# A dilated convolution with gate: a third level of differences for the V common part, the S part per oct, XB tiles by shifting, and another order of the units

## The chip, the core and the metric

The kernel runs on one core of one Trainium2 chip. The metric is the device time of one execution in microseconds. The kernel before takes 330.51 us (median of 3 runs, 329.73 to 330.65).

## The reference

The input x is 2 x 16000 x 144 (B x T x D) in bf16. A causal convolution with 15 taps and dilation 2 maps the 144 channels to 288; the first 144 of these go through tanh and the other 144 through a sigmoid, the two are multiplied, and the product is multiplied with a 144 x 144 matrix.

```python
pad = (K - 1) * dil                      # 28
xp = jnp.pad(x, ((0, 0), (pad, 0), (0, 0)))
h = sum over i of einsum('btc,cd->btd', xp[:, pad - 2 * i : pad - 2 * i + T, :], w[i])   # K = 15 taps
f, g = h[..., :D], h[..., D:]
z = jnp.tanh(f) * sigmoid(g)
return z @ w_o
```

(The loop over the taps is written as one line here.)

## The kernel before

**Tiles.** The 32000 time steps are laid out as 128 partitions of 250 consecutive steps (L = 250). A "tile" e is the set of the 128 steps that have the same place e in their partition, so one matmul with a 128x128 tile as its stationary operand gives 128 outputs for the 288 columns of a tap. Tap i at tile e needs tile e - 2i. Eight tiles make an oct; there are 31 octs and two steps before them. The first 128 channels of x are the A part: XA[slot, i] is tile i of an oct, transposed (channels on the partitions). The other 16 channels are the B part: one XB tile holds the 16 channels of eight tiles (e, e - 4, e - 8 and so on, 16 partitions each), so that two matmuls with the weights WB do the B part of all 15 taps.

**Fewer matmuls by differences.** Plain code would need 15 + 2 matmuls for each tile. The kernel uses a scheme in the manner of Winograd or Karatsuba: it forms sums of weights once (WS, WC, WT, WD, by `wsum`, line 655) and differences of tiles on VectorE, and combines the partial results. Of an oct it forms V and D(D) (first and second differences between tiles of even and odd place and neighbouring octs; `ef` and `vdiff`), DU (differences of XA, `diff`), BD (differences of XB); all of these go through line 709. For a pair of octs (o0 = 2m + 1, o1 = 2m + 2) `g_diffs` (line 774) forms differences between octs: GX of XA, GU of DU (both line 783), and GD of D (line 790).

**Units.** The main loop runs over 30 units (m, r), with 15 pairs m and r = 0, 1. A unit gives eight output tiles, four for each oct of the pair (h = 0, 1). Its parts, each with its matmuls on TensorE (all go through the helper at line 795), are:

- CD (line 979, k = 0, 1): common part from D with the weights WD, 8 matmuls in all; ScalarE evicts it to UD (k = 0) or UC (k = 1).
- XC (k = 0, 1): common part from DU with WT, 4 matmuls; ScalarE copies the result to a second PSUM bank (`copy`, line 937).
- XR (k = 0, 1): adds GU and XB parts for each oct, 12 matmuls; for k = 0 VectorE adds UD and writes UE (line 964, kept in the memory of Xp), for k = 1 ScalarE evicts to XS.
- UP (line 972, h = 0, 1): GpSimd adds UC and XS to UX (line 974). It also waits for an instruction of EF that is kept in TRIG.
- SC: the half that the S part of both octs shares, from XA with WT, 2 matmuls, and one copy to the other oct's bank.
- SR (h = 0, 1): adds the GX parts, 4 matmuls, and one copy each to the bank for the second half of the columns' pair.
- EF (line 1010, h = 0, 1): adds 4 V tiles in each of two banks, 16 matmuls; then four adds on VectorE (line 1023), two with UE into new banks, two with UX in place.
- DD (line 1028; h, part): adds the GD and BD parts, 23 matmuls in all; then `finish_pair`: sigmoid and tanh on ScalarE into TS (lines 472 and 475), the product on VectorE into Z (line 823).

That is 69 matmuls a unit. For each oct, `ship` (line 873) has the DMA transpose Z to ZT (line 878), `project` (PJ in the order; matmuls at line 895) multiplies by w_o in three groups, ScalarE evicts to OS (line 899), and a DMA stores it (line 905).

**Order.** Inside a unit the parts are issued in the order of the string `ORDER` (line 17). In it EF and DD belong to the present unit, and XC, CD, XR, SC, SR, UP to the next one; PJ takes the next group from a list. A list scheduler, `_Graph.schedule`, then plans all engines with a duration given for each operation, may move TensorE's groups forward within a window of `PE_WIN` = 14 groups, and gives out the 8 PSUM banks. VectorE operations and GpSimd's UX that are marked `lock` are kept from overlapping in the plan. The engines then run the planned order with semaphore waits.

**Loading.** For two pairs ahead, `stage` loads the x rows in chunks of 16 tiles (`load_xchunk`, Xr, three buffers). `load_xa` (line 672) copies the 128 A channels of an oct from Xr to a staging tile STA (on ScalarE up to oct 4, line 677, then on VectorE, line 680), and SP issues a DMA transpose to XA (line 682). `compact_chunk` copies the 16 B channels of a chunk into XBc, ordered so that the window of an XB tile is contiguous; `load_xb` (line 685) copies the eight windows of an oct to STB (line 698) and SP issues a DMA transpose to XB (line 700). STA and STB have one buffer each. XB has six slots of an oct, XA nine. All these DMAs are issued by SP, in the planned order.

Before the first unit, the outputs of the first tiles are computed directly with 17 matmuls each.

Of the kernel before, what the change touches and what calls it, by code (L numbers as in the profile page):

```python
# [16 lines left out]
ORDER = "EF0 DD01 PJ XC1 DD00 CD1 CD0 XR1 XC0 EF1 PJ SC UP1 DD10 XR0 PJ SR0 SR1 UP0 DD11"  # L17
# [357 lines left out]
def _conv_wavenet_kernel(nc, x, w, w_o, out):  # L375
# [17 lines left out]
    MB = (NE_ALL + 2) // 4 + 1  # L393
# [8 lines left out]
    NX = 3  # L402
# [7 lines left out]
    NST = 1  # L410
# [3 lines left out]
    STA_ACT = 4  # L414

    with contextlib.ExitStack() as st:
# [5 lines left out]
        XBc = sb("XBc", [NP, 4, MB, DB], BF16)  # L422
        STA = sb("STA", [NP, NST, 8, 128], BF16)
        STB = sb("STB", [NP, NST, 8, 128], BF16)
# [16 lines left out]
        GX = sb("GX", [NP, NG, 2, 2, 128], BF16)  # L441
# [3 lines left out]
        XS = sb("XS", [NP, 1, 2, N2], F32)  # L445
        UD = sb("UD", [NP, NUD, 2, N2], F32)
# [5 lines left out]
        WD = sb("WD", [NP, 4, 2, N2], BF16)  # L452
        Z = sb("Z", [NP, NZ, 8 * D], BF16)
# [113 lines left out]
        def cmp_op(eng, src, e0, e1, keys_r, tag, dur):  # L567

            m0, nm = (e0 + 2) // 4, (e1 - e0) // 4
            def f(v):  # L570
                s = src.rearrange("p (m c) d -> p c m d", c=4)
                dst = bass.AP(XBc[:].tensor, (MB - 1 - m0) * DB, [[4 * MB * DB, NP], [MB * DB, 4], [-DB, nm], [1, DB]])
                if eng == "act":
                    return v.activation(dst, s, ACT.Copy)
                return v.tensor_copy(dst, s)
# [9 lines left out]
        def compact_pro(pi):  # L585
            e0, e1 = pro_pieces[pi]
            if pi == 0:
                def f2(a):
                    s = Xp[:, 0:2, DA:D]
                    dst = bass.AP(XBc[:].tensor, 2 * MB * DB + (MB - 1) * DB, [[4 * MB * DB, NP], [MB * DB, 2], [1, DB]])  # L590
# [37 lines left out]
        def b_halo():  # L628
# [6 lines left out]
            def fix(p):  # L635
                s = Xp[:, H:E0, DA:D]
                dst = bass.AP(XBc[:].tensor, 2 * MB * DB + (MB - 1 - H // 4) * DB, [[4 * MB * DB, NP], [MB * DB, 2], [1, DB]])
                return p.tensor_copy(dst, s)
            g.add("pool", fix, r=xp_keys[2], w=hk, dur=0.3)
            for o, tiles, bb in ((-1, range(E0 - 4, E0), 7), (0, range(E0, E0 + 8), 6)):  # L640
                fns = []
                for e in tiles:
# [5 lines left out]
                      r=[("bank", HB[bb])], w=[("XB", bslot(o))], dur=0.5 if o < 0 else 0.95)  # L648
# [17 lines left out]

        def compact_chunk(ci):
            a, c = CH[ci]
            s = ci % NX
            cmp_op("dve", Xr[:, s, 0:c - a, DA:D], E0 + a, E0 + c, [("Xr", s)], ("XBc", ci), 0.16 + (c - a) * DB / 1900.0)  # L670

        def load_xa(o):
            s, q = aslot(o), o % NST
            ci = chunk_of(8 * o)
            i0 = 8 * o - CH[ci][0]
            if o <= STA_ACT:
                g.add("act", lambda a: a.activation(STA[:, q, :, :], Xr[:, ci % NX, i0:i0 + 8, 0:DA], ACT.Copy),
                      r=[("Xr", ci % NX)], w=[("STA", q)], dur=0.95, prio=2)
            else:
                g.add("dve", lambda v: v.tensor_copy(STA[:, q, :, :], Xr[:, ci % NX, i0:i0 + 8, 0:DA]),  # L680
                      r=[("Xr", ci % NX)], w=[("STA", q)], dur=0.34, lock=True)
            g.add("sp", lambda e: e.dma_start_transpose(XA[:, s, :, :], STA[:, q, :, :].rearrange("p a b -> p (a b)")),
                  r=[("STA", q)], w=[("XA", s)], dur=1.3, dma="xa", nbytes=8 * 128 * 128 * 2)

        def load_xb(o):
            s, q = bslot(o), o % NST
            e0 = E0 + 8 * o
            ck = set()
            for e in range(e0 - 28, e0 + 8):
                if e >= EP:  # L690
                    ck.add(("XBc", chunk_of(e - E0)))
                else:
                    ck.update(hk5 + ["XBcz"])
            m4 = (e0 + 2) // 4

            def cp(v):
                src = bass.AP(XBc[:].tensor, (MB - 1 - m4) * DB, [[4 * MB * DB, NP], [-DB, 2], [MB * DB, 4], [1, 128]])
                return v.tensor_copy(STB[:, q, :, :].rearrange("p (h c) b -> p h c b", h=2), src)  # L698
            g.add("dve", cp, r=sorted(ck, key=str), w=[("STB", q)], dur=0.34, lock=True)
            g.add("sp", lambda e: e.dma_start_transpose(XB[:, s, :, :], STB[:, q, :, :].rearrange("p a b -> p (a b)")),  # L700
                  r=[("STB", q)], w=[("XB", s)], dur=1.3, dma="xb", nbytes=8 * 128 * 128 * 2)

        def xbk(o):
            return [("XB", bslot(o))]
# [590 lines left out]
```

## Time and profile before

| | |
|---|---|
| median of 3 runs | 330.51 us |
| the profiled execution | 331.81 us |
| its span, first to last instruction | 330.1 us |
| TensorE, VectorE, ScalarE, GpSimd busy | 319.2, 305.6, 255.7, 107.2 us |
| weight loads busy | 250.4 us |
| mean granted TensorE clock | 0.998 |
| HBM read, written | 11.82, 9.22 MB |

The profile comes from one execution; the 1.7 us between its time and its span lie ahead of the first and behind the last instruction. "Busy" is the union of an engine's instructions; matmuls are pipelined, so that one is drawn 286 ns long while the next starts after about 122 ns. In the views PE is TensorE, PEld its weight loads, DVE VectorE, ACT ScalarE, POOL GpSimd, SP the engine that issues the DMAs; L795 is line 795 of the kernel. An arrow "<-" behind idle time names what ended it.

### The profile page before, as it was taken

What the parts mean: (1) busy time and instruction counts of PE and PEld (TensorE: products, weight loads), DVE (VectorE), ACT (ScalarE), POOL (GpSimd) and SP (SyncE); (2) the same over time, 40 slices, a digit from 0 to 9 for tenths busy, and PEclk for the clock granted to TensorE, in tenths of its full rate; (3) what the DMA queues carried; (4) which work ended last, traced back from release to release, by engine and by line L of the source; (5) the groups of instructions that cost most, each with busy time, mean ns of one, the idle gap of its engine ahead of it and who ended that gap; (6) DMA issues with size and microseconds to landing.
All of it is one profiled execution on the core that took longest, in us unless ns stands there. A gap on an engine that the chain in (4) does not pass through costs nothing. (4 is left out here: it accounts for less than half of the span.)

```text
span 330.1 us, 7585 instructions
## 1 busy us (share of the span) xinstructions
PE 319.2 (97%) x2701; PEld 250.4 (76%) x2701; DVE 305.6 (93%) x713; ACT 255.7 (77%) x786; POOL 107.2 (32%) x89
## 2 busy tenths in 40 slices
PE   7999799999999999999999999999999999999995
PEld 7877577888876778886788888887678878777873
DVE  2989899999999999999999999999999999999671
ACT  4455597898877878887789888877878788888875
POOL 7840333333213332223434322333312334331320
PEclk9999999999999999999999999999999999999999
DMA  8989714869475595838649495666847176463254
GB/s 205 320 129 201 182 32 113 199 101 193 108 151 138 135 174 126 175 113 148 168 84 224 103 164 157 135 167 137 171 106 161 51 160 105 104 134 73 71 75 143
DMA packets 111587, 46.51 MB, mean 141 GB/s; under 512 B 102766, under 2 KB 105247, under 8 KB 111549
## 3 DMA queue, kind: packets, MB, share of 16 engines
q1 hardware_dynamic: 111033, 45.68, 62.9%
q8 instruction: 21, 0.34, 0.5%
q0 software_dynamic: 512, 0.33, 0.4%
q14 instruction: 17, 0.14, 0.1%
q10 hardware_dynamic: 4, 0.01, 0.0%
HBM read 11.82 MB, written 9.22 MB: 64 GB/s over the span
## 5 line engine op out<-in xcount | busy, mean ns | idle before, releaser
L974 POOL TENSOR_TENSOR UX<-UC,XS 128x576 f32<-128x576 f32 x60 | 91.1, 1539 | 204.7 <-DVE PS L1023 166.9
L795 PE MATMUL PS<-WA,GD 128*128 128x288 bf16 x450 | 89.2, 286 | 2.5 <-DVE PS L1023 2.4
L795 PE MATMUL PS<-WB,BD 128*128 128x288 bf16 x240 | 67.4, 286 | 0.0
L795 PE MATMUL PS<-WC,V 128*128 128x288 bf16 x420 | 66.2, 286 | 0.2 <-ACT PS L937 0.2
L937 ACT ACTIVATE PS<-PS 128x288 f32<-128x288 f32 x150 | 58.5, 402 | 9.8 <-DVE Xp L964 3.4
L899 ACT ACTIVATE OS<-PS 128x432 bf16<-128x432 f32 (+1 forms) x91 | 44.4, 490 | 27.6 <-PE PS L895 26.4
L475 ACT ACTIVATE TS<-PS 128x144 bf16<-128x144 f32 x272 | 56.9, 298 | 8.6 <-PE PS L795 7.6
L1023 DVE TENSOR_TENSOR PS<-PS,Xp 128x288 f32<-128x288 f32 x120 | 53.6, 459 | 3.8 <-PE PS L795 2.8
L795 PEld LDWEIGHTS PS<-WA,GD 128*128 128x128 bf16 x450 | 40.6, 98 | 17.4 <-DVE PS L1023 5.5
L1023 DVE TENSOR_TENSOR PS<-PS,UX 128x288 f32<-128x288 f32 x120 | 49.8, 455 | 0.2
L795 PEld LDWEIGHTS PS<-WC,V 128*128 128x128 bf16 x420 | 40.9, 98 | 10.7 <-ACT PS L937 0.5
L472 ACT ACTIVATE TS<-PS 128x288 bf16<-128x288 f32 x114 | 39.8, 420 | 9.4 <-PE PS L795 9.2
L895 PE MATMUL PS<-WOR,ZT 128*128 128x144 bf16 (+1 forms) x333 | 44.5, 253 | 2.1 <-DVE Xp L964 2.0
L964 DVE TENSOR_TENSOR Xp<-PS,UD 128x576 f32<-128x576 f32 x60 | 43.0, 749 | 1.5 <-PE PS L795 1.1
L795 PE MATMUL PS<-WS,GU 128*128 128x288 bf16 x210 | 44.4, 286 | 0.0
L823 DVE TENSOR_TENSOR Z<-TS 128x288 bf16<-128x288 bf16 x125 | 36.7, 302 | 4.3 <-ACT TS L475 3.2
L795 PE MATMUL PS<-WB,XB 128*128 128x288 bf16 x140 | 37.6, 286 | 0.0
L895 PEld LDWEIGHTS PS<-WOR,ZT 128*128 128x128 bf16 x333 | 28.7, 98 | 9.5 <-DVE Xp L964 2.6
L795 PE MATMUL PS<-WD,DD 128*128 128x288 bf16 x210 | 34.6, 286 | 0.0
L709 DVE TENSOR_TENSOR BD<-XB 128x1024 bf16<-128x1024 bf16 (+1 forms) x35 | 28.6, 819 | 0.0
L795 PEld LDWEIGHTS PS<-WB,BD 128*128 128x128 bf16 x240 | 23.5, 98 | 5.7
L795 PE MATMUL PS<-WT,DU 128*128 128x288 bf16 x120 | 24.6, 286 | 0.9 <-DVE Xp L964 0.5
(85 smaller groups left out, 449.9 us busy)
## 6 DMA issues: line engine op xcount, KB each, us to landing
Xr<-in_x_dram SPq DMA_DIRECT2D x15, 576.0 KB, 4.5
out_dram<-OS SPq DMA_DIRECT2D x30, 288.0 KB, 2.2
WA<-in_w_dram SPq DMA_DIRECT2D x2, 288.0 KB, 5.1
ZT<-Z SPq DMA_TRANSPOSE x32, 3.1
Xp<-in_x_dram SPq DMA_DIRECT2D x2, 252.0 KB, 4.8
XA<-STA SPq DMA_TRANSPOSE x30, 3.1
XB<-STB SPq DMA_TRANSPOSE x30, 3.2
Xp<-in_x_dram SPq DMA_DIRECT2D x1, 441.0 KB, 4.0
```

Of the source, the lines that this page charges most:

```text
L472: return e.activation(bass.AP(t[:].tensor, off + (0 if st > 0 else n), [[row, NP], [st, 2], [1, n]]), bass.AP(PS[:].tensor, lo * 512 + c0, ...
L475: ins = e.activation(bass.AP(t[:].tensor, off + i * n, [[row, NP], [1, n]]), bass.AP(PS[:].tensor, q.phys * 512 + c0, [[8 * 512, NP], [1, ...
L709: return g.add("dve", lambda v: v.tensor_tensor(dst(), a(), b(), ALU.subtract), r=r, w=wk, dur=dur, prio=2, lock=True)
L795: return lambda t: t.matmul(bank(b), lhsT=lhs(), rhs=rhs(), start=start, stop=True, skip_group_check=True)
L823: return v.tensor_tensor(dst, TS[:, s, 1, :, :], TS[:, s, 0, :, :], ALU.mult)
L895: return t.matmul(PS[:, c0:c0 + n * D], lhsT=ZT[:, zt, blk_, :], rhs=WOR[:, wi_:wi_ + n, :].rearrange("p a b -> p (a b)"), start=first, st ...
L899: g.add("act", lambda e: e.activation(OS[:, os_, a:c, :].rearrange("p e d -> p (e d)"), PS[:, bo.phys * 512:bo.phys * 512 + (c - a) * D], ...
L937: g.add("act", lambda e: e.activation(bank(c), bank(b), ACT.Copy), r=[("bank", b)], w=[("bank", c)], dur=0.29, prio=prio)
L964: return v.tensor_tensor(ue(u % NU, q, 0, 2).rearrange("p (v n) -> p v n", v=2), src, UD[:, u % NUD, :, :], ALU.add)
L974: op = g.add("pool", lambda p: p.tensor_tensor(UX[:, u % NU, h, :, :], UC[:, 0, :, :], bass.AP(XS[:].tensor, h * N2, [[2 * N2, NP], [0, 2] ...
L1023: op = g.add("dve", lambda e, dst=dst, src=src, ua=ua: e.tensor_tensor(bank(dst), bank(src), ua(), ALU.add), r=[("bank", src), ("UX", us, ...
```

## The change

1. **V common part.** A new part CV (4 matmuls) computes, for the bank pairs of CD, V of o0 and of o0 - 2 with new weight sums WV, and ScalarE copies each result to a second bank; CD then accumulates on top of it. EF therefore needs only differences of V between octs, the new tile GV (formed in `g_diffs`), two matmuls in each bank in place of four.
2. **S part.** SC goes. SR computes an oct's S part from four XA tiles with the weights WC, four matmuls for each h in place of two; GX goes.
3. **XB by shifting.** Only 128 columns an oct (8 tiles x 16 channels) are compacted (C16), transposed (T16, one block) and stored to a scratch tensor in DRAM (s16). An XB oct is made of the oct before, moved up by 32 partitions by a DMA, and of two loads of 16 partitions each from s16. STB goes, and XBc, needed only at the start, lies in the memory of XS.
4. **STA** is loaded from x in DRAM by SP, in pieces of 128 channels, in place of the copies; it has two buffers. Xr has two buffers in place of three.
5. **Order.** The string `ORDER` changes; CV is added. UX waits for the first matmul group of EF in place of its first add, and its planned duration is 1.43 in place of 1.35.

A unit has 4 (CV) + 8 (CD) + 4 (XC) + 12 (XR) + 8 (SR) + 8 (EF) + 23 (DD) = 67 matmuls.

```diff
-ORDER = "EF0 DD01 PJ XC1 DD00 CD1 CD0 XR1 XC0 EF1 PJ SC UP1 DD10 XR0 PJ SR0 SR1 UP0 DD11"
+ORDER = "EF0 DD01 PJ EF1 XC1 DD10 DD00 DD11 CV CD1 XR1 UP0 XC0 CD0 XR0 SR0 PJ UP1 SR1 PJ"
...
-    NX = 3
+    NX = 2
...
-    NST = 1
+    NST = 2
...
         def load_xa(o):
             s, q = aslot(o), o % NST
-            ci = chunk_of(8 * o)
-            i0 = 8 * o - CH[ci][0]
-            if o <= STA_ACT:
-                g.add("act", lambda a: a.activation(STA[:, q, :, :], Xr[:, ci % NX, i0:i0 + 8, 0:DA], ACT.Copy),
-                      r=[("Xr", ci % NX)], w=[("STA", q)], dur=0.95, prio=2)
-            else:
-                g.add("dve", lambda v: v.tensor_copy(STA[:, q, :, :], Xr[:, ci % NX, i0:i0 + 8, 0:DA]),
-                      r=[("Xr", ci % NX)], w=[("STA", q)], dur=0.34, lock=True)
+            g.add("sp", lambda e: e.dma_start(STA[:, q, :, :], bass.AP(x_t, (KD + 8 * o) * D, [[L * D, NP], [D, 8], [1, DA]])),
+                  w=[("STA", q)], dur=0.5, dma="sta", nbytes=2 * NP * 8 * DA * 2)
...
         def load_xb(o):
...
-            g.add("dve", cp, r=sorted(ck, key=str), w=[("STB", q)], dur=0.34, lock=True)
-            g.add("sp", lambda e: e.dma_start_transpose(XB[:, s, :, :], STB[:, q, :, :].rearrange("p a b -> p (a b)")),
-                  r=[("STB", q)], w=[("XB", s)], dur=1.3, dma="xb", nbytes=8 * 128 * 128 * 2)
...
+            g.add("sp", lambda e: e.dma_start_transpose(T16[:, q, :], C16[:, ci % NX, c0:c0 + 128]), r=[("C16", ci % NX)], w=[("T16", q)], dur=1.3, dma="xb", nbytes=32768)
+            xdma(lambda: bass.AP(S16, 8 * o * DB * 128, [[128, NP], [1, 128]]), lambda: T16[:, q, :], [("T16", q)], [("S16", o)], 32768)
+            xdma(lambda: flatr(32, 96, s, 0, 8), lambda: flatr(0, 96, bslot(o - 1), 0, 8), xbk(o - 1), [("XB", s, 0)], 196608)
+            xdma(lambda: rows(0, DB, s, 0, 8), lambda: s16(8 * o, 8), [("S16", o)], [("XB", s, 3)], 32768)
+            if o > 1:
+                xdma(lambda: rows(16, DB, s, 0, 8), lambda: s16(8 * o - 4, 8), [("S16", o - 1), ("S16", o)], [("XB", s, 1), ("XB", s, 2)], 32768)
...
         def g_diffs(m):
...
+            def fv(v):
+                a1, am, a0 = (vslot(q) * 8 * TR for q in (o1, o0 - 1, o0))
+                A = bass.AP(V[:].tensor, a1, [[NV * 8 * TR, NP], [am - a1, 2], [4 * TR, 2], [1, 2 * TR]])
+                C = bass.AP(V[:].tensor, a0, [[NV * 8 * TR, NP], [0, 2], [4 * TR, 2], [1, 2 * TR]])
+                return v.tensor_tensor(GV[:, gslot(m), :, :, :], A, C, ALU.subtract)
...
+        def CV(u):
+            m, r, o0, o1 = octs(u)
+            CB[u] = [_pair(), _pair()]
+            for v in range(2):
+                b, c = CB[u][0][v], CB[u][1][v]
+                g.add("pe", [mm(b, lambda v=v: V[:, vslot(o0), v, r, :], lambda v=v: WV[:, 0, v, :], True),
+                             mm(b, lambda v=v: V[:, vslot(o0 - 2), v, r, :], lambda v=v: WV[:, 1, v, :], False)],
+                      r=[("V", vslot(o0)), ("V", vslot(o0 - 2)), ("WV", 0), ("WV", 1)], w=[("bank", b)], dur=2 * MM)
+                copy(b, c)
...
         def CD(u, k):
             m, r, o0, o1 = octs(u)
-            bs = _pair()
+            bs = CB[u][k]
...
-        def SC(u):
-            m, r, o0, o1 = octs(u)
-            UB[u] = [_pair(), _pair(), None, None]
-            p, q = UB[u][0][0], UB[u][1][0]
-            common(p, lambda: XA[:, aslot(o0), r, :], lambda: XA[:, aslot(o0 - 2), r, :], 0, [("XA", aslot(o0)), ("XA", aslot(o0 - 2))])
-            copy(p, q)
...
         def SR(u, h):
...
-            g.add("pe", [mm(p, lambda: GX[:, gslot(m), 1 - h, r, :], w0, False), mm(p, lambda: GX[:, gslot(m - 1), 1 - h, r, :], w1, False)],
-                  r=[("GX", gslot(m)), ("GX", gslot(m - 1))] + [("WC", 0, i) for i in range(4)], w=[("bank", p)], dur=2 * MM)
+            g.add("pe", [mm(p, lambda i=i: XA[:, aslot(o - i), r, :], wc(0, i), i == 0) for i in range(4)],
+                  r=[("XA", aslot(o - i)) for i in range(4)] + [("WC", 0, i) for i in range(4)], w=[("bank", p)], dur=4 * MM)
             copy(p, p1)
...
         def EF(u, h):
...
-                g.add("pe", region(p[v], [(lambda o_=o - i, v=v: V[:, vslot(o_), v, r, :]) for i in range(4)], [wc(1, i) if v == 0 else fc(i) for i in range(4)]),
-                      r=[("V", vslot(o - i)) for i in range(4)] + [("WC", 1 + v, i) for i in range(4 - v)] + [("WA", 0)], w=[("bank", p[v])], dur=4 * MM)
+                wv = [wc(1, i) if v == 0 else fc(i) for i in range(4)]
+                w0, w1 = (wv[1], wv[3]) if h == 0 else (wv[0], wv[2])
+                op = g.add("pe", [mm(p[v], lambda v=v: GV[:, gslot(m), 1 - h, v, r * 128:r * 128 + 128], w0, False),
+                             mm(p[v], lambda v=v: GV[:, gslot(m - 1), 1 - h, v, r * 128:r * 128 + 128], w1, False)],
+                      r=[("GV", gslot(m)), ("GV", gslot(m - 1))] + [("WC", 1 + v, i) for i in range(4 - v)] + [("WA", 0)], w=[("bank", p[v])], dur=2 * MM)
+                if v == 0:
+                    TRIG[0] = op
```

85 lines of the change are left out of this document (47 added, 38 removed).

## The prediction

> **What bounds the kernel now.** I read the page's busy line first, then the chain that ended last, then the stretches of the span, and last the groups.
>
> ```profile
> span 330.1 us, 7585 instructions
> PE 319.2 (97%) x2701; PEld 250.4 (76%) x2701; DVE 305.6 (93%) x713; ACT 255.7 (77%) x786; POOL 107.2 (32%) x89
> ```
>
> TensorE is busy nearly all the time, with VectorE close behind it. An average does not say which of them waits for which, so next comes the chain, in order of time (start, length, what, how many instructions):
>
> ```profile
> 299.06 4.53 PE PS L795 x37
> 303.60 0.37 PE PS L895 x4
> 303.97 2.21 PE PS L795 x18
> 306.17 0.25 PE PS L895 x3
> 306.42 1.72 PE PS L795 x14
> 308.13 0.37 PE PS L895 x4
> 308.50 4.53 PE PS L795 x37
> ```
>
> Here the chain is TensorE alone, and it repeats. One unit (half a pair of octs) is 37 + 18 + 14 = 69 matmuls of L795 and 4 + 3 + 4 = 11 projection matmuls of L895, and 308.50 - 299.06 = 9.44 us. A matmul costs 4.53 / 37 = 0.1224 us from start to start; the 69 take 8.46, the projections 0.99.
>
> ```profile
> 90.00:100.00 10.00, 9.37 (x80) 7.24 (x79) 10.00 (x23) 7.43 (x23) 2.46 (x3) 1.00 0.74 170
> 100.00:110.00 10.00, 9.23 (x77) 6.80 (x76) 10.00 (x22) 7.76 (x28) 2.92 (x3) 1.00 0.47 111
> 110.00:120.00 10.00, 9.26 (x79) 7.00 (x78) 9.97 (x24) 7.88 (x23) 2.61 (x2) 1.00 0.74 174
> 120.00:130.00 10.00, 10.00 (x88) 8.10 (x86) 9.93 (x24) 8.02 (x23) 3.19 (x3) 1.00 0.68 122
> 40.00:320.00 280.00, 275.98 (x2316) 216.86 (x2314) 272.45 (x630) 229.74 (x726) 87.89 (x58) 1.00 0.61 132
> 298.70:308.13 9.43, 9.43 (x82) 7.49 (x80) 9.17 (x22) 8.09 (x26) 3.23 (x2) 1.00 0.29 69
> 308.13:317.57 9.44, 9.44 (x83) 7.61 (x81) 5.81 (x16) 8.06 (x27) 2.77 (x2) 1.00 0.22 59
> ```
>
> Columns: stretch, its length, busy time of PE, PEld, DVE, ACT, POOL (instructions in brackets), granted clock, DMA share, GB/s. In the fourth row PE is full, and DVE nearly so (9.93). From 90 to 120 DVE is full and PE loses 0.63 + 0.77 + 0.74 = 2.14 us: VectorE has run late there and TensorE waits. Over 280 us PE idles 280.00 - 275.98 = 4.02 us. So TensorE's count of matmuls sets a unit's length, and VectorE takes over now and then. In the last row, where no more tiles are prepared, DVE needs 5.81 us of a unit; preparing tiles fills it to the brim.
>
> **The change part by part.**
>
> *Matmuls.* A unit before: CD 8, XC 4, XR 12, SC 2, SR 4, EF 16, DD 23 = 69, as counted in the chain. After: CV 4, CD 8, XC 4, XR 12, SR 8, EF 8, DD 23 = 67. Two fewer in each of 30 units: 60 x 0.1224 = **7.35 us**. They lie on the path wherever PE is full, so I take all of it. A unit would be 9.44 - 0.245 = 9.20 us.
>
> *VectorE.* The staging copies and GX go, GV comes.
>
> ```profile
> L680 DVE COPY STA<-Xr 128x1024 bf16<-128x1024 bf16 x26 | 10.8, 417 | 0.0
> L698 DVE COPY STB<-XBc 128x1024 bf16<-128x1024 bf16 x30 | 13.0, 434 | 0.5 <-DMA XB<-STB 0.5
> L783 DVE TENSOR_TENSOR GX<-XA 128x512 bf16<-128x512 bf16 x16 | 9.1, 567 | 0.0
> ```
>
> ```profile
> 211.00 0.82 DVE L1023 TENSOR_TENSOR PS<-PS,UX 128x288 f32<-128x288 f32 x2
> 211.73 0.42 DVE L680 COPY STA<-Xr 128x1024 bf16<-128x1024 bf16 x1
> 212.06 0.42 DVE L709 TENSOR_TENSOR DU<-XA 128x512 bf16<-128x512 bf16 x1
> 212.40 0.68 DVE L709 TENSOR_TENSOR V<-XA 128x1024 bf16<-128x1024 bf16 x1
> 213.00 0.42 DVE L698 COPY STB<-XBc 128x1024 bf16<-128x1024 bf16 x1
> 213.33 0.68 DVE L709 TENSOR_TENSOR DD<-V 128x1024 bf16<-128x1024 bf16 x1
> ```
>
> The timeline shows that durations overlap, so start to start counts: an add into PSUM 0.73 / 2 = 0.365, STA 0.33, STB 0.33, a 512-wide difference (DU, the shape of GX) 0.34, a 1024-wide one (V, the shape of GV) 0.60. Per unit, with one oct a unit and GX and GV once in two: -0.33 - 0.33 - 0.17 + 0.30 = **-0.53 us**. The compaction copy keeps its size. A full unit falls from about 9.37 (9.93 of 10) to 8.84, below 9.20. The three weight sums for WV in place of one for WT come before the units, beside the direct matmuls, with PE full; without that cover about 0.7 us by the same rows.
>
> *ScalarE.* One copy more per unit (two in CV, none in SC):
>
> ```profile
> L937 ACT ACTIVATE PS<-PS 128x288 f32<-128x288 f32 x150 | 58.5, 402 | 9.8 <-DVE Xp L964 3.4 <-PE PS L795 1.8
> ```
>
> That row makes 8.09 + 0.40 = 8.49 of 9.20 us. Four staging copies early on go. It fits, with less room than before; its price, if ScalarE were last, is 0.40 a unit or 12 us.
>
> *The order.* EF0 and EF1 now stand together, with the four DDs right behind them, so eight adds (8 x 0.365 = 2.92 us) come in one burst, and then four pairs of sigmoid and tanh. TensorE has EF0 0.49, EF1 0.49, a projection 0.37 and 23 DD matmuls 2.82 us = 4.17 us for the time of the burst. From EF0's first half (0.25) over 2.92 to the last DD half (0.37) it is 3.54 us. So it is covered if the adds run back to back, with 0.6 us to spare: about one 1024-wide difference. I assume that this goes wrong in some units: between 0 and 0.60 a unit, I take 0.07 (2 us in all), nearest to the rows where PE is full.
>
> *GpSimd.* UX keeps its work; its trigger is EF's first matmul group and no longer its first add, some 0.4 us earlier. What it costs VectorE shows where they meet:
>
> ```profile
> 99.33 3.26 POOL L974 TENSOR_TENSOR UX<-UC,XS 128x576 f32<-128x576 f32 x2 [7.54 <-DVE PS L1023]
> ```
>
> ```profile
> 101.24 1.62 DVE L783 TENSOR_TENSOR GX<-XA 128x512 bf16<-128x512 bf16 x1
> ```
>
> A 512-wide difference takes 1.62 us instead of 0.42 while UX runs. The new order moves these meetings; I take zero, between -1.2 and +1.2 us in a unit that has one.
>
> *Transfers.* SP's own time:
>
> ```profile
> 209.37 0.34 SPq L905 DMA_DIRECT2D out_dram<-OS  x1
> 210.74 2.29 SPq L878 DMA_TRANSPOSE ZT<-Z  x1
> 213.08 1.30 SPq L682 DMA_TRANSPOSE XA<-STA  x1
> 214.43 1.34 SPq L700 DMA_TRANSPOSE XB<-STB  x1
> 215.81 0.58 SPq L514 DMA_DIRECT2D Xr<-in_x_dram  x1
> ```
>
> ```profile
> q1 hardware_dynamic: 111033, 45.68, 62.9%
> out_dram<-OS SPq DMA_DIRECT2D x30, 288.0 KB, 2.2
> XA<-STA SPq DMA_TRANSPOSE x30, 3.1
> ```
>
> Now per unit: 0.34 + 2.29 + 1.30 + 1.34 + 0.29 (Xr serves two octs) = 5.6 us at most of 9.44. The XB transpose goes; instead come a transpose of one 128x128 block (T16), its store to DRAM, a shift of 96 partitions and two loads of 16 rows: four plain issues at 0.34 to 0.58, T16 between 0.34 and 1.34, and the STA load, 1024 pieces of 256 bytes, between 0.58 and 1.34. SP's sum becomes 4.2 + 1.4 to 2.3 + 0.3 to 1.3 + 0.6 to 1.3 = 6.5 to 9.1 us of 9.20. T16, store and load follow each other (3.1 + 2.2 + 2.2 = 7.5 us) and everything queued behind a waiting issue waits too: ZT for the projections, XA for the differences, the output stores. XB has six slots and its tiles are asked for two pairs ahead, so I cost it at nothing; if that cover is gone, see the last rival.
>
> Here the Trainium skill speaks against the change: "DMA: Bandwidth & Descriptors", Specifications, wants pieces of at least 512 bytes and says that smaller ones are read, modified and written. No run here shows the price of a plain load in 256-byte pieces; by that rule, as an estimate, the STA load would move its bytes twice and take the length of two transposes, still beside the matmuls.
>
> *Start-up.* XA(1) and XA(2) no longer wait for the Xr chunk and ScalarE's copy. PE's one large gap there,
>
> ```profile
> 38.01 0.42 PE L795 MATMUL PS<-WA,GD 128*128 128x288 bf16 x2 [1.21 <-DVE PS L1023]
> ```
>
> may close or move: XB(1) now needs a chain of transfers. Zero, between -1.2 and +3.
>
> **Sum.** -7.35 (matmuls), -2 (half of the 4.02 us of idle PE, as VectorE has room), +2 (the burst) = -7.35. The profiled execution took 331.81 (330.1 and 1.7 around it), so 324.5 in a profile. The median of the runs shown, 330.51, lies 1.3 lower, so **323.2 us**.
>
> **Rivals.**
>
> *VectorE was the bound.* For: full DVE in three rows above. Then its relief counts, not the matmuls: PE's idle time goes as well, -7.35 - 4.0 and up to 2 at start-up: 317 to 319, say **318.5**. Against: PE full in the fourth row. The Trainium skill's "Perfetto Trace Analysis", Identifying the Most-Contended Engine, would lean this way: it judges TensorE by its weight loads, 76% here, and that leaves VectorE highest. The trace disagrees in the units: with no PE wait at all the weight loads are busy 7.49 of 9.43 us.
>
> *The burst is not covered* (the other side). Place: between EF0 and the first DD. A difference of 0.60 us that stands between the adds, or four pairs whose banks ScalarE frees late, stops TensorE; all eight PSUM banks are in use then. It decides from 0.245 us a unit, where it eats the saving. At 0.60 in every unit it is 18 - 7.35 = +10.7, 341; in two of three units 12 - 7.35: **335**.
>
> *The saving goes into ScalarE's extra copy and bank waits* and nothing is left: **330.5**. For: 8.49 of 9.20 us.
>
> *Tiles come late.* SP at 9.1 us and waiting through the 7.5 us chain would need more than 9.20 us a unit; at 10 us it is 0.56 more than now in 28 units: +16, **346**. Against: six slots of XB.
>
> **How the numbers follow.** Forecast 0.46 (319.5 to 328), VectorE the bound 0.24, nothing left 0.08, burst 0.17, late tiles 0.05. The range 316.5 to 333 leaves out late tiles, most of the burst case and the edge below. A measurement of this kernel can tell about 0.3% from no change. Faster by more than that: 0.46 + 0.24 + 0.03 = 0.73; within: 0.05; slower: 0.22.
>
> **What would show it.** Right: a unit in the chain of 67 + 11 matmuls and 9.2 us, PE idle under 4 us from 40 to 320, DVE below 97% in the units, SP's waits without effect on PE. The burst: PE waits for the DVE adds (EF's line) ahead of matmuls of GD. ScalarE: PE waits for the copy or the sigmoid line. Late tiles: DVE idle before V or BD, released by a DMA. A start-up that is longer by over 3 us would make the forecast wrong without touching the units.

## The result, and the profile after

The changed kernel takes **334.24 us** (median of 20 runs, 330.56 to 337.41), beside 330.38 us for the kernel before on the same chip: a ratio of 1.009, 95% interval 1.0066 to 1.0114. It is slower by about 1%. Ratios, here and below, leave out executions in a slower state (five of the 20 of after, from 335.54 us up), so they differ a little from quotients of the medians. The forecast was 323.2 us, the range 316.5 to 333. The runs of after spread over 6.9 us; those of before, on that chip, over less than 3.

The head of its page, for an execution of 332.38 us:

```profile
span 330.7 us, 7628 instructions
...
PE 315.0 (95%) x2641; PEld 241.8 (73%) x2641; DVE 286.9 (87%) x659; ACT 249.1 (75%) x769; POOL 111.0 (34%) x89
...
q1 hardware_dynamic: 131641, 55.52, 77.2%
```

60 matmuls fewer, VectorE 18.7 us less busy, and the DMA queue at 77.2% in place of 62.9%. The end of the chain that ended last repeats undisturbed units:

```profile
263.40 7.47 PE PS L808 x61
...
272.60 7.37 PE PS L808 x59
...
281.94 7.23 PE PS L808 x59
...
291.13 7.23 PE PS L808 x59
```

291.13 - 281.94 = 9.19 us: the predicted 9.20. Stretches of after (same columns as before: PE, PEld, DVE, ACT, POOL, granted clock, DMA share, GB/s):

```profile
50.00:55.00 5.00, 2.57 (x15) 1.61 (x16) 4.97 (x12) 1.36 (x7) 0.00 (x0) 0.83 0.75 168
285.94:304.33 18.39, 18.39 (x158) 14.53 (x156) 13.54 (x34) 15.13 (x45) 5.65 (x4) 1.00 0.26 66
40.00:300.00 260.00, 251.44 (x2087) 192.31 (x2086) 244.39 (x548) 210.50 (x661) 88.13 (x56) 0.99 0.81 173
```

The second row is two units with PE full, late in the span, where little is loaded (DMA share 0.26). The third is what the units are like on the whole: DMA share 0.81 where before had 0.63 over the same stretch, and PE idle for 8.6 us (before: 4.0). Where the time went, by the start of one matmul that each unit has once (GU with WA, in the timelines): the second of these 30 marks lies at 39.37 us before and 41.95 after (+2.58); 28 units from there take 9.67 us each before and 9.70 after, where the matmuls alone would take 9.44 and 9.20; from the last mark to the end 20.0 and 17.1 us (-2.9). So the units gain nothing: 6.4 us of stops in 28 units have become 14.2. ("Stops" are what a unit takes beyond its matmuls; idle PE is less, as PE counts as busy where matmuls only follow each other more slowly.)

Nearly half of that is one unit of 15.84 us, from 41.95. Its timelines, SP first, then VectorE, GpSimd and TensorE:

```profile
37.04 1.33 SPq L681 DMA_TRANSPOSE XA<-STA  x1
38.49 0.53 SPq L693 DMA_DIRECT2D XB<-XB  x1
39.07 1.08 SPq L693 DMA_DIRECT2D XB<-s  x2
40.19 0.43 SPq L693 DMA_DIRECT2D s<-T  x1
40.67 1.25 SPq L681 DMA_TRANSPOSE XA<-STA  x1
...
45.45 0.43 DVE L716 TENSOR_TENSOR DU<-XA 128x512 bf16<-128x512 bf16 x1 [1.87 <-DMA XA<-STA]
45.80 1.51 DVE L836 TENSOR_TENSOR Z<-TS 128x288 bf16<-128x288 bf16 x1
47.23 1.89 DVE L790 TENSOR_TENSOR GU<-DU 128x1024 bf16<-128x1024 bf16 x1
...
51.92 0.82 DVE L1048 TENSOR_TENSOR PS<-PS,Xp 128x288 f32<-128x288 f32 x2
...
45.70 2.87 POOL L987 TENSOR_TENSOR UX<-UC,XS 128x576 f32<-128x576 f32 x2 [4.17 <-ACT UC L474]
...
52.43 0.42 PE L808 MATMUL PS<-WA,GD 128*128 128x288 bf16 x2 [3.76 <-DVE PS L1048]
```

An XA tile is issued at 40.67, behind the pieces of XB; DU waits 1.87 us for it on VectorE, in order, with the adds behind it. What was held now meets UX (a product of 0.30 us takes 1.51, GU 1.89 in place of 0.68). The adds start at 51.92, PE stands for 3.76 us until 52.43, and about 1 us later matmuls follow each other every 0.24 us: the granted clock is 0.50 from 53.40 to 56.70 (0.83 on average over the row from 50 to 55). Later stops have another shape: the chain runs through late ZT tiles.

```profile
134.71 4.91 DMA ZT<-Z
...
192.87 3.77 DMA ZT<-Z
...
249.49 4.13 DMA ZT<-Z
```

The transfers, by the list of DMA issues of after (last column: median from issue to landing). Output stores took 2.2 us and XA 3.1 before:

```profile
out_dram<-OS SPq DMA_DIRECT2D x30, 288.0 KB, 3.1
STA<-in_x_dram SPq DMA_DIRECT2D x30, 256.0 KB, 3.7
ZT<-Z SPq DMA_TRANSPOSE x32, 3.5
XA<-STA SPq DMA_TRANSPOSE x30, 4.0
```

**Theories to test.** T: the transfers, the STA load above all, make tiles late, and what PE needs stands behind them on SP and VectorE. A: the new arithmetic and order cost what they save (the burst, VectorE, ScalarE). Two more came up on the way: P, the order that the list scheduler happens to find, and G, GpSimd's UX beside VectorE.

### The profile page after: what moved, and what is told of

Read it like the earlier page. It is cut to its first block, busy times and chain, and to the rows that moved or that the text cites. A ratio compares the mean times of both kernels' runs of the same rounds, so it can differ in the third digit from the quotient of the medians.

```text
span 330.7 us, 7628 instructions
## 1 busy us (share of the span) xinstructions
PE 315.0 (95%) x2641; PEld 241.8 (73%) x2641; DVE 286.9 (87%) x659; ACT 249.1 (75%) x769; POOL 111.0 (34%) x89
## 3 DMA queue, kind: packets, MB, share of 16 engines
q1 hardware_dynamic: 131641, 55.52, 77.2%
HBM read 21.64 MB, written 10.20 MB: 96 GB/s over the span
## 4 chain that ended last, share of the span: by engine, by line
PE 65%; DVE 10%; DMA 9%; ACT 6%; POOL 4%; SPq 3%; issue 2%; ACTq 0%; DVEq 0%
PE PS L808 58%; PE PS L908 7%; DMA ZT<-Z 4%; POOL UX L987 4%; DMA WA<-in_w_dram 3%; DVE PS L1048 3%; ACT TS L477 1%; ACT PS L950 1%; DMA s<-T 1%; DVE GU L790 1%; SPq L516 1%; ACT TS L474 1%; DVE V L716 1%; DMA XB<-XB 1%; DVE DD L716 1%
## 5 line engine op out<-in xcount | busy, mean ns | idle before, releaser
L987 POOL TENSOR_TENSOR UX<-UC,XS 128x576 f32<-128x576 f32 x60 | 95.3, 1608 | 207.2 <-ACT UC L477 131.1
L950 ACT ACTIVATE PS<-PS 128x288 f32<-128x288 f32 x180 | 75.3, 429 | 1.6 <-PE PS L808 1.5
L474 ACT ACTIVATE TS<-PS 128x288 bf16<-128x288 f32 x148 | 53.0, 420 | 27.5 <-PE PS L808 27.1
L477 ACT ACTIVATE TS<-PS 128x144 bf16<-128x144 f32 x204 | 44.2, 312 | 11.9 <-PE PS L808 11.4
L977 DVE TENSOR_TENSOR Xp<-PS,UD 128x576 f32<-128x576 f32 x60 | 42.8, 753 | 11.3 <-ACT UD L474 7.6
L1048 DVE TENSOR_TENSOR PS<-PS,Xp 128x288 f32<-128x288 f32 x120 | 49.5, 458 | 1.8 <-PE PS L808 1.2
L808 PE MATMUL PS<-WC,XA 128*128 128x288 bf16 x240 | 39.1, 286 | 0.0
L808 PE MATMUL PS<-WD,DD 128*128 128x288 bf16 x210 | 37.9, 286 | 0.1
L808 PE MATMUL PS<-WC,GV 128*128 128x288 bf16 x210 | 36.3, 286 | 0.2 <-ACT PS L950 0.2
L808 PEld LDWEIGHTS PS<-WC,XA 128*128 128x128 bf16 x240 | 22.3, 98 | 5.6 <-ACT TS L474 0.2
L808 PEld LDWEIGHTS PS<-WD,DD 128*128 128x128 bf16 x210 | 20.3, 98 | 6.7 <-ACT PS L950 0.9
```

Source lines behind the costliest of these rows:

```text
L474: return e.activation(bass.AP(t[:].tensor, off + (0 if st > 0 else n), [[row, NP], [st, 2], [1, n]]), bass.AP(PS[:].tensor, lo * 512 + c0, ...
L477: ins = e.activation(bass.AP(t[:].tensor, off + i * n, [[row, NP], [1, n]]), bass.AP(PS[:].tensor, q.phys * 512 + c0, [[8 * 512, NP], [1, ...
L808: return lambda t: t.matmul(bank(b), lhsT=lhs(), rhs=rhs(), start=start, stop=True, skip_group_check=True)
L950: g.add("act", lambda e: e.activation(bank(c), bank(b), ACT.Copy), r=[("bank", b)], w=[("bank", c)], dur=0.29, prio=prio)
L977: return v.tensor_tensor(ue(u % NU, q, 0, 2).rearrange("p (v n) -> p v n", v=2), src, UD[:, u % NUD, :, :], ALU.add)
L987: op = g.add("pool", lambda p: p.tensor_tensor(UX[:, u % NU, h, :, :], UC[:, 0, :, :], bass.AP(XS[:].tensor, h * N2, [[2 * N2, NP], [0, 2] ...
```

## The experiments

Each ran beside the kernel before (330.4 to 330.8 us).

### One part undone at a time

**math_only**: the new arithmetic and order and the two Xr buffers, but load_xa, compact_chunk and load_xb of before (copies to STA, XBc and STB, XB by one transpose; one weight sum lies in spare room of Xp).

```diff
-            g.add("sp", lambda e: e.dma_start(STA[:, q, :, :], bass.AP(x_t, (KD + 8 * o) * D, [[L * D, NP], [D, 8], [1, DA]])),
+                g.add("dve", lambda v: v.tensor_copy(STA[:, q, :, :], Xr[:, ci % NX, i0:i0 + 8, 0:DA]),
...
-            g.add("sp", lambda e: e.dma_start_transpose(T16[:, q, :], C16[:, ci % NX, c0:c0 + 128]), r=[("C16", ci % NX)], w=[("T16", q)], dur=1.3, dma="xb", nbytes=32768)
+            g.add("sp", lambda e: e.dma_start_transpose(XB[:, s, :, :], STB[:, 0, :, :].rearrange("p a b -> p (a b)")),
```

> The change's arithmetic, order and trigger (67 matmuls a unit), with the loading of before: staging copies, STB, XB by a transpose of eight blocks; Xr has two buffers, and the sum of the B weights lies in spare room of Xp, so that it fits. Theory (the new loading brings the tiles late, at the start above all): the stall of 6.6 us before the third unit is gone and the units are 9.20 us, so 322 to 325 us. Rival (the order with eight adds in a burst stops TensorE): the loss stays, 330 to 335 us.

Measured 332.67 us (328.86 to 335.23), ratio 1.0028 (0.9996 to 1.006). T's range is missed and the burst's holds. In the profiled execution (335.23 us, its longest) VectorE is full from 70 to 300 us, PE idles for 8 us, and what it waits for most over the whole run is the adds (late XA tiles hold VectorE for 1.8 us in all):

```profile
70.00:300.00 230.00, 221.92 (x1839) 170.61 (x1837) 227.81 (x526) 185.37 (x559) 77.48 (x46) 0.99 0.66 139
...
PE PS L803 <- DVE PS L1043: 8.2, 8, 2.4
```

**load_only**: arithmetic and order of before (SC and GX back, CV, GV and WV out), both new loads.

```diff
-ORDER = "EF0 DD01 PJ EF1 XC1 DD10 DD00 DD11 CV CD1 XR1 UP0 XC0 CD0 XR0 SR0 PJ UP1 SR1 PJ"
+ORDER = "EF0 DD01 PJ XC1 DD00 CD1 CD0 XR1 XC0 EF1 PJ SC UP1 DD10 XR0 PJ SR0 SR1 UP0 DD11"
```

> The change's loading alone (STA from DRAM, XB by shifting, two Xr buffers, XBc in the memory of XS), with the arithmetic, the order and the trigger of before (69 matmuls a unit). Theory (loading): slower than before by the start-up loss, 335 to 342 us. Rival (the burst): no slower than before, 327 to 331 us, since VectorE has 0.66 us a unit less to do.

Measured 350.66 us, ratio 1.0596 (1.0567 to 1.0625): the direction of T, 9 us beyond its upper end. The waits of this kernel (total, times, longest) name ZT:

```profile
PEld PS L901 <- DMA ZT<-Z: 10.7, 8, 2.2
PE PS L901 <- DMA ZT<-Z: 8.2, 7, 1.9
```

**sta_direct_xb_old**: after, with compact_chunk and load_xb of before (a copy to STB, one transpose in place of T16, s16, shift and loads) and one STA buffer.

```diff
-            g.add("sp", lambda e: e.dma_start_transpose(T16[:, q, :], C16[:, ci % NX, c0:c0 + 128]), r=[("C16", ci % NX)], w=[("T16", q)], dur=1.3, dma="xb", nbytes=32768)
+            g.add("sp", lambda e: e.dma_start_transpose(XB[:, s, :, :], STB[:, 0, :, :].rearrange("p a b -> p (a b)")),
```

> The change, but XB by STB and a transpose of eight blocks as before; STA still straight from DRAM, with one staging buffer. Theory: if SP's chain of small transfers for XB is what delays the others, 322 to 326 us; if the STA loads are, 330 to 336 us. Rival (the burst): 330 to 335 us.

Measured 342.35 us, ratio 1.0344 (1.0311 to 1.0376): above all three of its ranges. **xb_shift_sta_copy**: after, with STA by the copies, three Xr buffers and one STA buffer.

```diff
-    NX = 2
+    NX = 3
...
-    NST = 2
+    NST = 1
...
-            g.add("sp", lambda e: e.dma_start(STA[:, q, :, :], bass.AP(x_t, (KD + 8 * o) * D, [[L * D, NP], [D, 8], [1, DA]])),
+                g.add("dve", lambda v: v.tensor_copy(STA[:, q, :, :], Xr[:, ci % NX, i0:i0 + 8, 0:DA]),
```

> The change, but STA by copies from Xr as before (ScalarE up to oct 4, then VectorE), with one staging buffer and three Xr buffers; XB by shifting. Theory: if the chain for XB is what delays, 330 to 336 us; if the STA loads are, 322 to 326 us. Rival (the burst): 330 to 335 us.

Measured **325.95 us** (324.61 to 327.8), ratio 0.986 (0.9825 to 0.9894), faster than both kernels, in the range for the STA loads. From 70 to 300 us PE is all but full, and most units take 9.19 to 9.20 us:

```profile
70.00:300.00 230.00, 229.15 (x1934) 179.29 (x1932) 220.44 (x521) 191.54 (x577) 79.33 (x50) 1.00 0.64 148
```

It still loses some 4 us in two units of 11.3 us at the start, where VectorE waits in order, ahead of UX's adds, for an XB tile, and PE waits for the adds:

```profile
41.22 0.69 DVE L723 TENSOR_TENSOR BD<-XB 128x1024 bf16<-128x1024 bf16 x1 [1.26 <-DMA XB<-s]
41.83 0.82 DVE L1055 TENSOR_TENSOR PS<-PS,UX 128x288 f32<-128x288 f32 x2
...
42.34 0.42 PE L815 MATMUL PS<-WA,GD 128*128 128x288 bf16 x2 [2.59 <-DVE PS L1055]
```

### Less traffic in the same order

Each kernel above is planned anew, so its whole order differs. The next two keep the order of after on every engine; STA's load alone differs. **after_sta_eighth** (from oct 3 on it loads one tile of eight and leaves the others out):

```diff
-            g.add("sp", lambda e: e.dma_start(STA[:, q, :, :], bass.AP(x_t, (KD + 8 * o) * D, [[L * D, NP], [D, 8], [1, DA]])),
+            n8 = 8 if o <= 2 else 1
+            g.add("sp", lambda e: e.dma_start(STA[:, q, 0:n8, :], bass.AP(x_t, (KD + 8 * o) * D, [[L * D, NP], [D, n8], [1, DA]])),
```

> The changed kernel with every instruction in its place, but from oct 3 on an STA load moves one tile of eight (128 pieces of 256 bytes in place of 1024), so that the other tiles are stale and the output is not the reference's. Theory (the traffic of the STA loads makes the other transfers land late): the waits for ZT go, the DMA share falls from 0.81 to about 0.65, 325 to 329 us. Rival (SP's queue and the planned order, whatever the traffic): 332 to 335 us as the changed kernel. Rival (the burst of adds): no change either.

**after_sta_2k** (the same bytes in 2-KB pieces, which are not the elements that the computation needs):

```diff
-            g.add("sp", lambda e: e.dma_start(STA[:, q, :, :], bass.AP(x_t, (KD + 8 * o) * D, [[L * D, NP], [D, 8], [1, DA]])),
+            g.add("sp", lambda e: e.dma_start(STA[:, q, :, :].rearrange("p a b -> p (a b)"), bass.AP(x_t, (KD + 8 * o) * D, [[L * D, NP], [1, 8 * DA]])),
```

> The changed kernel with every instruction in its place, but an STA load takes 2048 contiguous bytes a partition (128 pieces) in place of eight pieces of 256; it loads other elements than the computation needs, so the output is not the reference's. Theory (it is the count of small pieces that costs): as good as moving an eighth, 325 to 329 us. If the bytes count: 330 to 333 us. Rival (the planned order or the burst): 332 to 335 us.

One tile of eight: 328.51 us, ratio 0.9928 (0.9902 to 0.9954), **5.7 us less than after** (5.4 by the ratios), and the unit of 15.84 takes 11.41. The same bytes in pieces of 2 KB: 331.59 us, ratio 1.0019 (0.9999 to 1.004), 2.6 us less, in the range for the bytes: the small pieces are less than half of it. The stretch, the queue and PE's waits with one tile of eight (after waited 5.5 us for the adds and 2.3 for ZT):

```profile
70.00:300.00 230.00, 226.47 (x1895) 173.78 (x1894) 216.49 (x493) 189.70 (x593) 77.65 (x48) 1.00 0.70 151
q1 hardware_dynamic: 106553, 49.10, 67.8%
...
PE PS L809 <- DVE PS L1049: 3.2, 7, 0.9
...
PE PS L909 <- DMA ZT<-Z: 1.1, 2, 0.8
```

This is shown for T: the traffic of the load by itself (seven eighths of it) costs 5.7 us. But 328.51 is not 323. These two runs keep every issue on SP, and SP is nearly full: by its timelines its issues take 97.4 of the 190 us from 70 to 260 in before, 169.3 in after and 165.8 with one tile of eight (from 30 to 70 us: 18.8, 37.0 and 37.0 of 40). No run in this order takes issues away.

### Other plans of the same operations

**after_lat40** and **stacopy_lat40** (after, and the kernel of 325.95 us, planned with a latency nearer to what the transfers show):

```diff
-DMA_LAT = 2.3
+DMA_LAT = 4.0
```

> The changed kernel, but the list scheduler plans with 4.0 us of DMA latency in place of 2.3, nearer to what the trace shows (STA 3.7, XA 4.0, ZT 3.5 to landing); nothing else differs, but every engine's order is planned anew. Theory (VectorE, in order, is held by tiles that land later than planned): the start-up stall of 6.6 us shrinks to under 3 and the ZT waits go, 322 to 328 us. Rival (the burst): 331 to 336 us.

> XB by shifting, STA by copies from Xr (the kernel that gave 325.95), planned with 4.0 us of DMA latency. Theory: its start-up loss (two units of 11.3 us in place of 9.2) shrinks, 321 to 325 us. Rival (these units are slow for another reason than landing times): 325 to 328 us.

337.85 us, ratio 1.0205 (1.0179 to 1.023), and 326.98, ratio 0.9878 (0.9862 to 0.9893). Neither gained, and after_lat40 lies above both its ranges: nothing here supports that the plan merely assumes too short a latency, though it is one plan each. **stacopy_other_plan** changes only a duration in the plan, and with it the order of every engine; **stacopy_lat_early** and **stacopy_margin** try to mend the start and the meetings with UX. One edit each, in this order:

```diff
-MM = 0.122
+MM = 0.1225
```

```diff
-                op.end = dma_free + DMA_LAT
+                op.end = dma_free + (4.0 if 15.0 < st < 60.0 else DMA_LAT)
```

```diff
-                port[e] = st + op.base
+                port[e] = st + op.base + 0.5
```

> The kernel with 325.95 us (XB by shifting, STA by the copies) planned with 0.1225 us for a matmul in place of 0.122: the same operations, another order on every engine. It tells how much the plan alone moves the time. Theory: under 2 us, 324 to 328 us, so that the 8.3 us between this loading and the direct load of STA are no accident of the plan. Rival (orders differ by as much as the edits): 329 us or more, or 322 or less.

> The kernel with 325.95 us, planned with a transfer latency of 4.0 us in place of 2.3 only for transfers issued between 15 and 60 us of the plan. In its first units VectorE waits in order for an Xr chunk (0.99 us) and an XB tile (1.26 us) with adds queued behind, and PE waits 2.59 and 1.87 us for the adds. Theory: the plan puts the adds ahead of what lands late, and of some 4.5 us lost in the first units 2 to 4 come back: 322 to 324 us. Rival (the tiles are needed by PE at that time anyway, or the chain of transfers on SP is as long as before): 325 to 328 us.

> The kernel of 325.95 us, planned so that a locked VectorE operation and UX keep 0.5 us apart in both directions, where the plan so far puts them end to end. Theory (collisions after small delays are what costs): 321 to 325 us. Rival (another order is another draw, as between 325.95 and 340.66 us): 327 us or more.

340.66 us (ratio 1.0263, 1.0219 to 1.0307), 332.35 (1.0049, 1.0025 to 1.0073) and 333.47 (1.0077, 1.0049 to 1.0105). The rival held in the first and the last; stacopy_lat_early came out slower than either of its ranges. **Five plans of the same operations give 325.95, 326.98, 332.35, 333.47 and 340.66 us**, a spread of 14.7 us, twice the saving that was forecast. The differences between the newly planned kernels above therefore do not by themselves say what an edit costs; those in one order do. The profiled execution of stacopy_other_plan (345.24 us, its longest) shows the kind of its stops:

```profile
100.67 1.20 DVE L686 COPY STA<-Xr 128x1024 bf16<-128x1024 bf16 x1 [0.93 <-DMA XA<-STA]
101.78 1.88 DVE L723 TENSOR_TENSOR V<-XA 128x1024 bf16<-128x1024 bf16 x1
...
104.82 0.53 PE L915 MATMUL PS<-WOR,ZT 128*128 128x144 bf16 x4 [2.24 <-DVE Xp L984]
```

```profile
105.00:112.00 7.00, 6.47 (x41) 4.33 (x39) 5.88 (x16) 3.77 (x13) 0.00 (x0) 0.76 0.55 160
```

A VectorE copy waits 0.93 us for a transfer, then it and V run beside UX (1.20 and 1.88 us in place of 0.42 and 0.68), PE stands 2.24 us, the clock over the next 7 us is 0.76: a unit of 13.97 us.

### Arithmetic and order

**xb_shift_old_math** (load_only with the copies to STA), and **stacopy_spread_order** (the kernel of 325.95 us with the order of before):

```diff
-ORDER = "EF0 DD01 PJ EF1 XC1 DD10 DD00 DD11 CV CD1 XR1 UP0 XC0 CD0 XR0 SR0 PJ UP1 SR1 PJ"
+ORDER = "EF0 DD01 PJ XC1 DD00 CV CD1 CD0 XR1 XC0 EF1 PJ UP1 DD10 XR0 PJ SR0 SR1 UP0 DD11"
```

> The arithmetic and order of before (69 matmuls a unit, SC and GX, no CV) with XB by shifting and STA by the copies: the same loading as the run with 325.95 us, so that the difference of the two is what the new arithmetic and order are worth under the loading that suits them. Theory: TensorE sets a unit, so this run is slower by the 60 matmuls, 7.35 us, and stands at 331 to 335 us, about the time of before, though VectorE has more room. Rival (VectorE was the bound of before, and XB by shifting alone brings the gain): 324 to 327 us, and the new arithmetic is worth nothing.

> The new arithmetic, XB by shifting and STA by the copies, but the parts of a unit in the order of before, with CV in place of SC ahead of CD: EF1 and its adds stand half a unit behind EF0 again. Theory: in the steady units the burst of eight adds is covered (9.20 us with the new order), so the order of before gains nothing there: 325 to 329 us, and no unit shorter than 9.19 us. Rival (the burst costs time, above all in the first units, where PE waits 2.6 and 1.9 us for the adds): 320 to 323 us.

334.89 us (1.0122, 1.0097 to 1.0146): inside its theory's band, but with plans differing by 14.7 us one draw proves little. 351.89 us (1.0649, 1.061 to 1.0687): outside both its ranges, and no sign that the spread order is a cure. Undisturbed units with the burst take 9.20 us, so the burst alone costs nothing; where VectorE is full besides, as in math_only, PE waits for the adds, and no run in one order separates the two.

### UX taken out of VectorE's way

Same order on every engine, with 36 of UX's 288 columns (the other columns are set to zero once, ahead of the first addition, and their sums left out), in after, in stacopy_other_plan, in before, in after with an eighth of the STA load, and in the kernel of 325.95 us:

```diff
-            op = g.add("pool", lambda p: p.tensor_tensor(UX[:, u % NU, h, :, :], UC[:, 0, :, :], bass.AP(XS[:].tensor, h * N2, [[2 * N2, NP], [0, 2], [1, N2]]), ALU.add),
+            op = g.add("pool", lambda p: p.tensor_tensor(UX[:, u % NU, h, :, 0:36], UC[:, 0, :, 0:36], bass.AP(XS[:].tensor, h * N2, [[2 * N2, NP], [0, 2], [1, 36]]), ALU.add),
...
+            if u == 0 and h == 0:
+                PRE[op] = lambda p: p.memset(UX[:, :, :, :, 36:N2], 0.0)
...
```

> The kernel after with the same order on every engine; GpSimd's UX (line 987) adds only 36 of the 288 columns, once it has set the others to zero ahead of its first addition (the sums of the common parts are left out in 7 of 8 columns). Theory: a tile or a row chunk that lands 1 to 2 us late holds VectorE in order, the held differences then run beside UX and take 1.9 us in place of 0.68, and so the adds come 3 to 4 us late; without the long UX the unit of 15.84 us shrinks to 12 or less, and the kernel to 324 to 328 us. Rival (the late tiles alone make the stops): the unit stays above 14 us and the kernel at 331 us or more.

> The kernel of 340.66 us (XB by shifting, STA by the copies, planned with 0.1225 us a matmul) with the same order on every engine, and UX on 36 of 288 columns as in the run beside it (the rest of the sums left out). Its plan has three stops of 4.8 to 7.1 us. Theory (the plans differ by how often late transfers meet UX): the stops fall to under 3 us and the kernel to 325 to 330 us. Rival: 336 us or more, the plan loses time elsewhere.

> The kernel before, same order, UX on 36 of 288 columns in the same way (the rest of the sums left out). Its units average 9.67 us where 9.44 is the matmuls' time, 6.4 us over in all. Theory: part of this is UX beside VectorE, which is full in those units: 325 to 328 us. Rival: UX costs it nothing, 329.5 to 331 us.

After: 333.52 us (1.0059, 1.0026 to 1.0092), 0.7 us less than after, with overlapping intervals: no gain is shown, and the theory's range is missed. The stop at 42 us shrinks (10.45 us) as the theory says, but waits for ZT come in its place. After's own waits, then those of the run:

```profile
PE PS L808 <- DVE PS L1048: 5.5, 6, 3.8
...
PE PS L908 <- DMA ZT<-Z: 2.3, 3, 1.1
...
DVE DU L716 <- DMA XA<-STA: 1.9, 1, 1.9
```

```profile
PE PS L908 <- DMA ZT<-Z: 9.4, 5, 2.8
...
PE PS L808 <- DVE PS L1051: 0.6, 2, 0.4
```

The other plan: 330.72 us (0.9999, 0.9979 to 1.0019), 9.9 us less, two thirds of what this plan is slower than the one of 325.95; the rest stays. Before: **324.19 us** (0.9783, 0.9741 to 0.9824), 6.6 us less. Before's stretch as it is, then with the short UX:

```profile
70.00:300.00 230.00, 225.98 (x1894) 177.28 (x1893) 227.40 (x524) 187.60 (x585) 72.73 (x48) 1.00 0.65 140
```

```profile
70.00:300.00 230.00, 229.87 (x1947) 184.53 (x1945) 223.88 (x536) 192.97 (x605) 16.26 (x48) 1.00 0.65 140
```

PE's 4 us of idle time there are down to 0.13, its 28 units average 9.44 us, and VectorE is busy 294.3 us in place of 305.6: all that before loses in the units is UX beside a VectorE without slack. Its DMA share of 0.65 then makes no stop.

> The kernel after, same order on every engine, with both reductions: from oct 3 on the STA load moves one tile of eight (the other tiles keep old values), and UX adds 36 of 288 columns (the rest of the sums left out). The load alone gave 328.51 us, the short UX alone 333.52 us, where PE's waits for the adds fell from 5.5 to 0.6 us and those for ZT rose from 2.3 to 9.4 us. Theory (two bounds beside each other: transfers that come late, and differences stretched beside UX; each is only seen when the other is gone): nearly all units at 9.20 us, 317 to 321 us, against 324.19 us of before with the short UX, so that the 60 matmuls' 7.35 us less about 2.6 us at the start show. Rival (the plan loses time in a third place): 324 us or more.

> The kernel of 325.95 us (STA by copies, XB by shifting, whole transfers), same order, with UX on 36 of 288 columns (the rest of the sums left out). Theory (its 4 to 5 us over in the first units are differences held by late XB and XA tiles and then stretched beside UX): 319 to 322 us. Rival (the transfers by themselves hold PE there, or ZT comes late in place of the adds, as after with the short UX): 324 us or more.

After with both reductions: 328.32 us (0.9931, 0.9906 to 0.9957). The rival held, something is left, and beside the short load the short UX gains nothing (328.51 without it). The kernel of 325.95 us: 325.35 (0.9837, 0.9819 to 0.9855), the rival too: its start stays, held by XA, XB and Xr. What is left in after with both reductions, from the timelines of SP, TensorE and VectorE, and a stretch behind the first stop (the profiled execution took 330.01 us, its longest):

```profile
90.58 2.35 SPq L694 DMA_DIRECT2D XB<-s  x2
...
97.93 0.54 PE L909 MATMUL PS<-WOR,ZT 128*128 128x144 bf16 x4 [1.99 <-DMA ZT<-Z]
...
221.72 0.23 DVE L674 COPY C<-Xr 128x256 bf16<-128x256 bf16 x1 [1.83 <-DMA Xr<-in_x_dram]
...
222.59 0.82 DVE L1052 TENSOR_TENSOR PS<-PS,UX 128x288 f32<-128x288 f32 x2
```

```profile
100.00:103.90 3.90, 3.90 (x25) 2.73 (x23) 2.41 (x7) 2.76 (x9) 0.00 (x0) 0.71 0.80 207
```

Two issues for XB take SP 2.35 us (1.08 in the row of after further up), ZT goes out behind them and is 1.99 us late for PE (unit of 13.03 us, clock 0.71); a compaction copy waits 1.83 us for its row chunk with the adds behind it (unit of 10.97 us). These are transfers again, XB's pieces, ZT and Xr, now with an eighth of the STA load.

## Why the prediction was wrong

**The failed step is "Transfers", which the sum put at nothing**: XB because it "has six slots and its tiles are asked for two pairs ahead, so I cost it at nothing", and the STA load because it stays "beside the matmuls". Shown in its place: the STA load's traffic by itself costs 5.7 us, in one order, of the 11 us between 323.2 and 334.24. How a late transfer reaches TensorE in spite of the slots is seen in the traces: VectorE stops in order at the first difference or copy of the late tile (1.87 us for XA at 45.45), with the adds behind it; on SP, ZT and XA go out behind the other issues. The bound of 6.5 to 9.1 us of SP a unit was sound: 169.3 of 190 us is 8.6 us of a unit of 9.70, 5.0 in before. The rival "tiles come late" had this mechanism, with a chance of 0.05, and mis-sized it: +16 us, everywhere, where it is single stops. What the nearly full SP and XB's own pieces cost beside the STA traffic is argued from the traces, not shown.

- *Matmuls, -7.35*: right where it can be seen (9.19 us a unit, PE full). By the marks 28 units save 6.9 us of matmuls, and stops eat it.
- *VectorE*: right in size (18.7 us over 30 units is -0.62 each; -0.53 was forecast). "-2, half of the idle PE": wrong. In before that idle time was UX beside a full VectorE (6.6 us); in after PE idles longer, and there a short UX gives back about 0.7 us, within the noise. *GpSimd, zero*: not refuted in after's order; in the plan of 340.66 us UX cost 9.9 us, 0.35 a unit and inside the bound of 1.2.
- *The burst, +2*: did not show in undisturbed units. Its sign, PE waiting for the adds ahead of GD, did appear (5.5 us in six stops); 3.76 us of it came from a late XA tile and UX. The sign could not tell the two apart. With the loading of before, in math_only, the sign appeared with hardly a late tile (8.2 us, in its longest execution), so the burst beside a full VectorE stays a rival there.
- *ScalarE*: right, no bound; 249.1 us busy.
- *Start-up, zero*: wrong by 2.58 us, just within its bound of +3, plus the long unit behind it. One tile of eight does not change the 2.58 (the mark stays at 41.95); its cause is open.
- *Small pieces*: the Trainium skill's "DMA: Bandwidth & Descriptors", Specifications, wants pieces of at least 512 bytes for the full rate. The direction agrees: pieces of 256 bytes in place of 2 KB cost 2.6 us here. Of the estimate of twice the bytes there is no sign: a load's landing is 3.7 us against 3.2, and the reads from HBM rise by 9.8 MB (11.82 to 21.64), what the STA loads (7.86) and XB's loads (1.95) hold once.
- *The sum*: the profiled run should have been 324.5 and was 332.38, 7.9 more: 7.8 from the units (14.2 of stops where 6.4 were kept), 2.6 from the start, less 2.4 at the end. The other 3.2 lie in the median, which I set 1.3 under the profile as before and which lies 1.9 above it, with executions spread over 6.9 us; why they spread so is not shown.
- *The range* took the plan for given. Five plans of one set of operations spread over 14.7 us; no step allowed for that.

**What stays open.** With both reductions in the same order after takes 328.32 us; before with the short UX, less 7.35, plus 2.58 at the start, would be 319.4. The 8.9 us between are seen in the trace as stops for ZT, Xr and XA (three units of 10.5 to 13.0 and two longer ones at the start, 9.7 us over together, in the longest execution), but no run in that order left XB's own transfers or SP's added issues out, so their share is argued, not shown. Which of two plans loses less can't be told ahead from these runs.

## What to carry to other kernels

A transfer that "has slots" still costs time if what waits for it stands in order ahead of work that the bound engine needs: look at what is queued behind each wait, on the issuing queue too. Before one credits an edit under a list scheduler, compare in one order (shrink a transfer or an operation, keep the order), and plan the same operations several times to see the spread. Here the best kernel is the change without its direct STA load, **325.95 us**, 1.4% under before, in one plan out of five; the plan is part of that result.

## What the runs showed of the hardware that was not expected

- A stop of TensorE can cost more than its length. After the stops of 3.76 us (after), 2.24 (stacopy_other_plan) and 1.99 (after with both reductions) matmuls ran at full pace for 1 to 2 us and then 0.24 us apart in place of 0.122 for about 3.3 us: the granted clock is 0.50 from 53.40 to 56.70, from 106.95 to 110.25 and from 98.90 to 102.20 us of these runs. That is some 14 matmuls at 0.12 us more, 1.6 us by these rows. It does not always come: in the kernel of 325.95 us the stop of 2.59 us (and one of 1.87 us) left the clock at 1.00 (from 42.30 to 52.30 and from 50 to 58 us). What decides is not shown.
- Loads in 256-byte pieces, as estimates from the queue's share: its time falls from 0.772 x 330.7 = 255.3 us to 0.678 x 326.3 = 221.2 without 24.5 loads' worth of STA pieces, 1.39 us of all 16 engines for 256 KB, or 22 ns a piece on one. In 2-KB pieces it is 0.732 x 329.7 = 241.3 us, 0.47 less per load.
- A short UX frees 6.6 us in before, though GpSimd is busy for a third of the span only: what counts is the VectorE time that it takes (11.3 us less busy) where VectorE has none to spare. Operations on tiles in SBUF are stretched (GU 0.68 to 1.89 us); adds that read PSUM are not (three in 1.20 us at 38.72 in after, with UX running from 38.77).
